# Loading the q and k rows of two tiles at a time, turning them by heads, and taking four blocks of the first product whole

## The chip, the cores and the metric

The kernel runs on one core of one Trainium2 chip. The metric is the device time of one execution in microseconds; the time quoted is the median of three runs. Engine names are those of the profile: PE is the matrix engine (PEld its weight loads), DVE the vector engine, ACT the scalar engine, POOL the GpSimd engine, SP the engine that here only issues DMAs.

## The reference

B=8 sequences of S=576 tokens; q, k and v have H=8 heads of 64. Attention stays within chunks of 64 tokens, its result (tokens by 512) goes through a gated two-layer product with a three-tap convolution over the tokens:

```
scores = 0.125 * q_c @ k_c.T             # per batch, head, chunk of 64
attn   = exp(scores - max); attn = attn / (sum(attn) + 1e-9)
x      = (attn @ v_c), heads side by side            # 4608 x 512
h      = maximum(x @ w_in, 0)                        # 512 -> 1024
conv   = sum over k of conv_w[k] * h[token + k - 1]  # zeros at each end of a batch
out    = (h * sigmoid(conv)) @ w_out                 # 1024 -> 512
```

## The kernel before

**Tiles and units.** The 4608 tokens are 36 tiles of 128 tokens (two chunks each). Four tiles make a unit of 512 tokens, u = 0 to 8. d_ff is cut into eight blocks f of 128. For each unit and block, `mm1(u, f)` (L337) makes h, and after ReLU, convolution and gate (L344 to L417) `mm2(u, j, f)` (L469) adds to the four output tiles j. Both products split each operand into a high and a low part and add three products, so a block of `mm1` over 512 tokens is 4 x 3 matmuls of 512 columns. The parts of x come from `x_hi` (L326, ACT) and `x_lo` (L329, DVE); the weights are split on the chip, in pieces of 512 or 1024 columns a partition: load L497, `w_scale` (L512, ACT), `w_shift` (L516), `w_words` (L521), then the high part (L557 and L563) and the low part (L525).

**Attention of a tile.** q and k have to stand with the head dimension on the partitions. For tiles 0 to 4 (`t < NP`) `load_rows` (L111 to L118) puts two consecutive tokens of each head into one packet of 512 bytes, q on the even partitions and k on the odd ones; `t_pe` (L169) turns them with matmuls against the identity, eight matmuls (16 records in the trace, as fp32 runs in two passes) for each half, a half being all heads of the even or of the odd tokens; `t_copy` (L189) copies each half from PSUM into the tile's `qkT` (every other element is written). Tiles 5 to 8 are loaded a token a row and turned by PE transposes (L181, copies L194); later tiles are turned by DVE (L201). Then come `scores` (L208, matmuls L215), `s_max` (L225) and `s_sub` (L229) on DVE, `s_exp` (L238) on ACT, `s_sum` (L245), `s_eps` (L248) and `s_rec` (L251) on DVE, the normalising product on POOL (L277), `p_pe` (L284) which turns the weights of attention, its copy `p_copy` (L289), `attn_v` (L303), and `x_hi` and `x_lo`.

**Unit 0.** Its `mm1` blocks are all cut into two halves of 256 columns, since the first needs only tiles 0 and 1 and the second tiles 2 and 3. Every step before the first `mm1` lies ahead of the dense stage; PE is then given small filler matmuls on the identity (L1018 with 512 columns, L1021 with 128) at places that the program works out.

**What sets the order.** Each piece of work is a `step(...)` with an engine, its predecessors, and resources that it takes and frees (PSUM banks, buffers). A table `order_` (L833) lists all steps in the order in which they are written out; `moved_` names steps that run on another engine than usual. Each engine works through its own instructions strictly in that order, and each DMA goes out through SP's queue in that order. The costs and lags in the `step` calls only set the begin times by which buffers, banks and fillers are chosen.

## Time and profile before

| what | value |
|---|---|
| median of three runs | 471.08 us (470.34, 471.23, 471.08) |
| profiled execution, its time | 470.57 us |
| profiled execution, its span | 468.8 us |
| PE busy | 460.9 us (98%) |
| DVE busy | 350.3 us (75%) |
| first `mm1` matmul starts | 27.39 us |
| last PE instruction ends | about 465.4 us |

Times in the rows are microseconds from the span's start. The busy share of PE is of records, fillers included; PE's matmuls are pipelined, so that the distance between the starts of neighbouring groups tells what a group takes, and their busy times overlap a little.

### The profile page before, as it was taken

The page shows a single profiled execution, that of the slowest core. Times are in us where ns is not written, and L with a number is a line of the kernel's source. Part 1 is how long each engine was busy: PE and PEld are TensorE (multiplying, and loading weights), DVE is VectorE, ACT ScalarE, POOL GpSimd, SP SyncE. Part 2 cuts the span into 40 slices and gives each one's busy share as a digit, 9 for nine tenths or more (in the row PEclk, how much of TensorE's full clock was granted, in tenths as well). Part 3 has the DMA queues.
Part 4 walks back from the last instruction along what each step waited for, and adds up shares of the span by engine and source line. Part 5 has one row for each costly group of instructions (what it writes and reads, how often), then busy time and mean ns, then how long its engine had stood idle before and what let it go on. Part 6 is the DMA issues. An engine that isn't in the chain of part 4 may idle for free.

```text
span 468.8 us, 10873 instructions
## 1 busy us (share of the span) xinstructions
PE 460.9 (98%) x4373; PEld 384.1 (82%) x4373; DVE 350.3 (75%) x632; ACT 226.6 (48%) x522; POOL 184.6 (39%) x256
## 2 busy tenths in 40 slices
...
GB/s 212 250 317 247 279 81 128 149 95 95 96 110 146 135 57 72 167 89 146 101 144 78 67 135 154 119 1 70 60 99 3 45 1 112 46 1 69 1 22 112
DMA packets 175638, 50.53 MB, mean 108 GB/s; under 512 B 159180, under 2 KB 167908, under 8 KB 175588
## 3 DMA queue, kind: packets, MB, share of 16 engines
...
## 4 chain that ended last, share of the span: by engine, by line
PE 89%; DVE 9%; issue 2%; ACT 0%; POOL 0%; POOLq 0%; DVEq 0%; ACTq 0%
PE b_ps L469 42%; PE b_ps L337 37%; PE b_ps L215 3%; PE b_ps L303 3%; PE b_ps L176 2%; DVE wt L521 1%; DVE x_l L329 1%; DVE z L245 1%; DVE ww L521 1%; DVE m L225 1%; DVE wi_l L525 1%; DVE c L378 1%; DVE wt L516 1%; DVE e L229 1%; DVE c L394 1%
## 5 line engine op out<-in xcount | busy, mean ns | idle before, releaser
L469 PE MATMUL b_ps<-wo_h,g_h 128*128 128x512 f32 x288 | 113.8, 395 | 0.3 <-DVE x_l L329 0.3
L469 PE MATMUL b_ps<-wo_h,g_l 128*128 128x512 f32 x288 | 112.2, 390 | 0.0
L469 PE MATMUL b_ps<-wo_l,g_h 128*128 128x512 f32 x288 | 112.2, 390 | 0.0
L417 POOL TENSOR_TENSOR g_l<-c,g_h 128x510 fp32r<-128x510 f32 (+1 forms) x80 | 79.4, 998 | 75.4 <-DVE g_h L406 48.5
L378 DVE SCALAR_TENSOR_TENSOR c<-b_ps,cw,c 128x510 f32<-128x510 f32 x72 | 53.2, 740 | 37.4 <-ACT c L373 30.8
L337 PE MATMUL b_ps<-x_h,wi_h 128*128 128x512 f32 (+1 forms) x320 | 79.8, 371 | 0.0
L337 PE MATMUL b_ps<-x_l,wi_h 128*128 128x512 f32 (+1 forms) x320 | 78.8, 368 | 0.0
L337 PE MATMUL b_ps<-x_h,wi_l 128*128 128x512 f32 (+1 forms) x320 | 78.7, 368 | 0.0
L337 PEld LDWEIGHTS b_ps<-x_h,wi_h 128*128 128x128 f32 x320 | 56.5, 188 | 10.6 <-issue 0.3
L337 PEld LDWEIGHTS b_ps<-x_l,wi_h 128*128 128x128 f32 x320 | 56.9, 188 | 10.1
L337 PEld LDWEIGHTS b_ps<-x_h,wi_l 128*128 128x128 f32 x320 | 56.9, 189 | 10.0
L469 PEld LDWEIGHTS b_ps<-wo_h,g_h 128*128 128x128 f32 x288 | 54.0, 188 | 12.4 <-DVE x_l L329 0.7
L469 PEld LDWEIGHTS b_ps<-wo_h,g_l 128*128 128x128 f32 x288 | 54.1, 188 | 11.4
L469 PEld LDWEIGHTS b_ps<-wo_l,g_h 128*128 128x128 f32 x288 | 54.1, 188 | 10.7
L373 ACT ACTIVATE c<-b_ps,cw 128x510 f32<-128x510 f32 (+1 forms) x72 | 49.8, 693 | 23.0 <-DVE b_ps L348 19.1
L344 ACT ACTIVATE b_ps<-b_ps 128x512 f32<-128x512 f32 x56 | 32.4, 584 | 55.2 <-PE b_ps L337 54.7
L260 POOL TENSOR_TENSOR wt<-wt,z 128x512 f32<-128x512 f32 x28 | 29.2, 1050 | 75.7 <-DVE z L251 28.0
L390 ACT ACTIVATE c<-c 128x510 f32<-128x510 f32 (+1 forms) x72 | 45.5, 635 | 27.7 <-DVE c L384 27.4
L394 DVE SCALAR_TENSOR_TENSOR c<-c,b_ps 128x510 f32<-128x510 f32 (+1 forms) x72 | 48.6, 678 | 10.2 <-ACT c L390 8.1
L384 DVE SCALAR_TENSOR_TENSOR c<-b_ps,cw,c 128x510 f32<-128x510 f32 (+1 forms) x72 | 53.0, 740 | 1.6 <-ACT rim L363 0.4
L201 DVE STREAM_TRANSPOSE qkT<-qk 128x512 f32<-128x512 f32 (+1 forms) x60 | 37.9, 641 | 2.8 <-DMA qk<-in_k 1.5
L326 ACT CAST x_h<-b_ps 128x512 fp32r<-128x512 f32 x36 | 20.6, 590 | 39.6 <-PE b_ps L303 36.0
...
## 6 DMA issues: line engine op xcount, KB each, us to landing
out<-os SPq DMA_DIRECT2D x35, 256.0 KB, 2.3
...
v<-in_v SPq DMA_DIRECT2D x25, 256.0 KB, 3.3
w<-in_moe_w_out SPq DMA_DIRECT2D x4, 1024.0 KB, 7.3
...
w<-in_moe_w_in SPq DMA_DIRECT2D x2, 1024.0 KB, 7.0
```

Of the source, the lines that this page charges most:

```text
L201: nc.vector.transpose(out=turned(st)[:, i].rearrange("p g (n i) -> p g n i", i=32)[:, :, to:to + n], in_=groups[b, i][:, :, n0:n0 + n, :])
L260: nc.gpsimd.tensor_tensor(out=two(st, "to"), in0=two(st, "of"), in1=z, op=ALU.mult)
L326: nc.scalar.copy(out=x_view(t, x_h), in_=x_src(st))
L337: nc.tensor.matmul(banks[st["h"]][:, c0:c1], lhsT=wt[:, f // 2, kt, P * (f % 2):P * (f % 2) + P], rhs=xt[:, u % 2, kt, c0:c1], start=n == ...
L344: nc.scalar.activation(out=h, in_=h, func=AF.Relu)
L373: nc.scalar.mul(out=st["c"], in_=banks[st["h"]][:, i0:i0 + n], mul=cw[:, FT + f:FT + f + 1])
L378: nc.vector.scalar_tensor_tensor(out=c[:, a:n], in0=banks[st["h"]][:, i0 + a - 1:i0 + n - 1], scalar=cw[:, f:f + 1], in1=c[:, a:n], op0=AL ...
L384: nc.vector.scalar_tensor_tensor(out=st["c"], in0=banks[st["h"]][:, i0 + 1:i0 + 1 + n], scalar=cw[:, 2 * FT + f:2 * FT + f + 1], in1=st["c ...
L390: nc.scalar.activation(out=st["c"], in_=st["c"], func=AF.Tanh, scale=0.5)
L394: nc.vector.scalar_tensor_tensor(out=st["c"], in0=st["c"], scalar=1.0, in1=banks[st["h"]][:, i0:i0 + n], op0=ALU.add, op1=ALU.mult)
L417: nc.gpsimd.tensor_tensor(out=g_l[:, f, gs], in0=st["c"][:, cs], in1=g_h[:, f, gs].bitcast(F32), op=ALU.subtract)
L469: nc.tensor.matmul(banks[st["o"]], lhsT=gt[:, f, o:o + P], rhs=wt[:, f, :], start=f == 0 and n == 0, stop=f == FT - 1 and n == 2)
```

## The change

Tiles 1 and 2, and tiles 3 and 4, are loaded together (`PAIRS`): a partition takes four consecutive tokens of each head, 1024 bytes in one packet, 64 partitions for q and 64 for k. The pair 3 and 4 lies across the end of a batch and is loaded in four DMAs (48 and 16 partitions each of q and of k). The pair is turned by heads: `t_pe2` makes, for a group g of two heads, eight matmuls (one for each token of four and each head) into one bank, so a pair takes four banks instead of four halves; `t_copy2` copies a bank to the `qkT` of both tiles, reading PSUM with a step of 512 bytes and writing SBUF in one run. For that the two `qkT` buffers are now two views of one tile. Tile 0 is loaded and turned as before.

Blocks f = 2 to 5 of unit 0 are taken whole (`HALVED = (0, 1, 6, 7)`): 12 matmuls of 512 columns instead of 24 of 256, which then wait for all four tiles of x. `s_eps` may run on POOL. Lags of some loads are changed (they only move the chosen begin times), and the tables `order_` and `moved_` are new throughout.

```
+    HALVED = (0, 1, 6, 7)
     NP = 5
+    PAIRS = {1: 2, 3: 4}
...
+    qk_all = spots.tile([P, G, 2, 2, 2 * C], F32, name="qkT")
+    homes["qkT"] = [qk_all[:, :, :, n].rearrange("p g i c -> p i g c") for n in range(2)]
...
-            (b0, t0), (b1, t1) = chunk(2 * t), chunk(2 * t + 1)
+            e = 4 if t in PAIRS else 2
+            (b0, t0), n0 = chunk(2 * t), min(C, (S - chunk(2 * t)[1]) // e)
             for i, src in enumerate((q, k)):
-                for b, t_, p0, n in [(b0, t0, 0, C)] if b0 == b1 else [(b0, t0, 0, C // 2), (b1, t1, C // 2, C // 2)]:
-                    nc.sync.dma_start(out=r[i, p0:p0 + n], in_=src[b, :, t_:t_ + 2 * n, :].rearrange("h (p e) d -> p h (e d)", e=2))
+                for b, t_, p0, n in [(b0, t0, 0, n0)] + [(b0 + 1, 0, n0, C - n0)] * (n0 < C):
+                    nc.sync.dma_start(out=r[i, p0:p0 + n], in_=src[b, :, t_:t_ + e * n, :].rearrange("h (p e) d -> p h (e d)", e=e))
...
+    def t_pe2(st, g):
+
+        r = row_slot(st).rearrange("p (g u e d) -> p g u e d", g=G, u=2, e=4)
+        for e in range(4):
+            for u in range(2):
+                nc.tensor.matmul(banks[st["tp", g]][D * u:D * u + D, P * e:P * e + P], lhsT=r[:, g, u, e],
+                                 rhs=ident.rearrange("p (n two) -> p two n", two=2), start=True, stop=True)
...
+    def t_copy2(st, g, copy=nc.scalar.copy):
+        for st_ in st["sts"]:
+            turned(st_)
+        copy(out=qk_all[:, g].rearrange("p i x (n e) -> p i (x n) e", e=4), in_=banks[st["tp", g]].rearrange("p (e i m) -> p i m e", e=4, i=2))
...
+    def s_eps_g(st):
+        nc.gpsimd.tensor_scalar(out=st["z"], in0=st["z"], scalar1=1e-9, scalar2=None, op0=ALU.add)
...
+        if t in PAIRS:
+            parts = 2 if C * (2 * t % NCK) + 4 * C <= S else 4
+            st["sts"] = [st]
+            ld = step("SP", 0.63 * parts, load_key, load_rows, (st, t), lag=3.4 if parts == 2 else 3.7, n=parts)
+            tt = []
+            for g in range(G):
+                s = step("PE", 1.07, key - 3, t_pe2, (st, g), [ld], behind=[before.get("t")], take=[("bk", st, ("tp", g))] + [("qkT", t), ("qkT", t + 1)] * (g == 0))
...
+                tt.append(step("ACT", 0.62, key - 3, t_copy2, (st, g), [s], free=[("bk", st, ("tp", g))], alt=[dict(eng="DVE", cost=0.68, fn=t_copy2_v)]))
...
-        s = step("DVE", 0.17, key + 2, s_eps, (st,), [s], port=True)
+        s = step("DVE", 0.17, key + 2, s_eps, (st,), [s], port=True, alt=[dict(eng="POOL", cost=0.2, fn=s_eps_g, port=True)])
...
-        if u == 0:
+        if u == 0 and f in HALVED:
             s = step("PE", 1.43, key, mm1, (st, u, f, 0, UN // 2), wi_done[f] + [x_done[0], x_done[1]], take=[("bk", st, "h")])
...
     order_ = [
-        71, 72, 90, 0, 74, 91, 1, 73, 75, 3, 2, 77, 92, 78, 4, 5, 93, 109, 94, 110,
+        71, 72, 90, 0, 17, 73, 1, 127, 74, 75, 3, 77, 91, 78, 79, 4, 2, 5, 6, 80,
...
```

The loads at the start of SP's queue, before. The buffers r_108 to r_112 are the rows of tiles 0 to 4, `os` holds the convolution weights, `c` and `v` rows of v, w_123 the first large piece of w_in.

```order
L117 DMA r_108<-in_q 64x8x128
L117 DMA r_108<-in_k 64x8x128
L117 DMA r_109<-in_q 64x8x128
L117 DMA r_109<-in_k 64x8x128
L497 DMA os_70<-in_moe_conv_w 24x256
L117 DMA r_110<-in_q 64x8x128
L117 DMA r_110<-in_k 64x8x128
L117 DMA r_111<-in_q 64x8x128
L117 DMA r_111<-in_k 64x8x128
L117 DMA r_112<-in_q 32x8x128 x2
L117 DMA r_112<-in_k 32x8x128 x2
L147 DMA c_84<-in_v 64x4x64
```

The same place of SP's queue now; r_107 is tile 0, r_108 the pair 1 and 2, r_109 the pair 3 and 4, wi_112 and w_120 pieces of w_in.

```order
L122 DMA r_107<-in_q 64x8x128
L122 DMA r_107<-in_k 64x8x128
L122 DMA r_108<-in_q 64x8x256
L122 DMA r_108<-in_k 64x8x256
L521 DMA os_70<-in_moe_conv_w 24x256
L521 DMA wi_112<-in_moe_w_in 128x2x512
L122 DMA r_109<-in_q 48x8x256
L122 DMA r_109<-in_q 16x8x256
L122 DMA r_109<-in_k 48x8x256
L122 DMA r_109<-in_k 16x8x256
L521 DMA w_120<-in_moe_w_in 128x4x512
L152 DMA c_82<-in_v 64x4x64
```

A small piece of w_in now goes ahead of tiles 3 and 4, and the first large one ahead of all rows of v; before, both came behind the first rows of v.

On ACT, before, the stretch from the second half of tile 2 to the first large piece of w_in (`e` are the weights of attention, `pT` their turned form, the copies at L192 those of tiles 0 to 4).

```order
L192 COPY qkT_72<-b_ps 128x4x2x64
L238 ACTIVATE e_77<-e_77 128x512
L192 COPY qkT_73<-b_ps 128x4x2x64
L192 COPY qkT_72<-b_ps 128x4x2x64
L289 COPY pT_80<-b_ps 128x512
L289 COPY pT_81<-b_ps 128x512
L238 ACTIVATE e_76<-e_76 128x512
L238 ACTIVATE e_77<-e_77 128x512
L326 CAST x_h<-b_ps 128x4x128
L512 ACTIVATE wt_83<-w_123 128x1024
L192 COPY qkT_72<-b_ps 128x4x2x64 x2
L194 COPY qkT_73<-b_ps 128x512
```

The same stretch of ACT now (L215 are the copies of the pairs, L259 the exponentials, L536 `w_scale`).

```order
L259 ACTIVATE e_74<-e_74 128x512
L215 COPY qkT<-b_ps 128x512 x2
L536 ACTIVATE wt_81<-wi_112 128x512
L215 COPY qkT<-b_ps 128x512
L536 ACTIVATE wt_80<-w_120 128x1024
L259 ACTIVATE e_75<-e_75 128x512
L259 ACTIVATE e_74<-e_74 128x512
L215 COPY qkT<-b_ps 128x512 x4
L350 CAST x_h<-b_ps 128x4x128
L581 CAST wi_h<-wt_80 128x1024
L313 COPY pT_79<-b_ps 128x512
L207 COPY qkT<-b_ps 128x4x128
```

The first large `w_scale` stood behind the exponentials of tiles 2 and 3; now it stands ahead of those of tiles 1 and 2 and of the four copies of the pair 3 and 4.

On PE, before, from the first filler to the turning of the attention weights of tile 0 (L176 turns rows, L215 are scores, L284 turns the attention weights, L578 belongs to the convolution weights).

```order
L1018 MATMUL b_ps<-ident 128x512
L1021 MATMUL b_ps<-ident 128x128 x10
L176 MATMUL b_ps<-ident,r_108 64x128 x16
L176 MATMUL b_ps<-ident,r_109 64x128 x8
L215 MATMUL b_ps<-qkT_72 64x64 x16
L176 MATMUL b_ps<-ident,r_109 64x128 x8
L176 MATMUL b_ps<-ident,r_110 64x128 x8
L215 MATMUL b_ps<-qkT_73 64x64 x16
L176 MATMUL b_ps<-ident,r_110 64x128 x8
L578 MATMUL b_ps<-ident,wt_82 128x24
L176 MATMUL b_ps<-ident,r_111 64x128 x16
L284 MATMUL b_ps<-ident,e_76 128x128 x4
```

The same stretch of PE now, as far as the scores of tile 3 (L181 turns tile 0, L193 a pair, L236 are scores, L327 is the product with v).

```order
L1061 MATMUL b_ps<-ident 128x512
L1064 MATMUL b_ps<-ident 128x128 x5
L181 MATMUL b_ps<-ident,r_107 64x128 x16
L1064 MATMUL b_ps<-ident 128x128
L236 MATMUL b_ps<-qkT 64x64 x16
L193 MATMUL b_ps<-ident,r_108 64x128 x32
L602 MATMUL b_ps<-ident,wt_80 128x24
L308 MATMUL b_ps<-ident,e_74 128x128 x4
L236 MATMUL b_ps<-qkT 64x64 x32
L193 MATMUL b_ps<-ident,r_109 64x128 x32
...
L236 MATMUL b_ps<-qkT 64x64 x16
```

A pair is turned in one piece, its scores follow in one piece, and fewer fillers stand ahead of tile 0.

## Rows read from the trace of the kernel before

**Rows 1.** The head of the profile's page: span, and the busy time of three engines with its share of the span and the count of instructions.

```profile
span 468.8 us, 10873 instructions
PE 460.9 (98%) x4373; PEld 384.1 (82%) x4373; DVE 350.3 (75%) x632; ACT 226.6 (48%) x522; POOL 184.6 (39%) x256
```

**Rows 2.** Busy time of each engine by stage: the stretch, its length, then for each engine its busy time and count, then the granted clock, DMA's busy share and GB/s.

```profile
5.50:27.40 21.90, 20.12 (x449) 16.83 (x448) 17.53 (x38) 13.62 (x23) 4.17 (x4) 1.00 1.00 263
27.40:65.30 37.90, 36.83 (x505) 34.23 (x503) 37.59 (x64) 31.86 (x59) 17.42 (x20) 1.00 0.83 236
65.30:440.00 374.70, 374.70 (x3302) 309.87 (x3303) 285.54 (x516) 171.54 (x420) 155.73 (x214) 1.00 0.54 89
```

**Rows 3.** The waits of PE over the whole span: the waiting line, what it waited for, the sum, how often, the longest.

```profile
PE b_ps L284 <- POOL e L277: 1.5, 2, 0.9
...
PE b_ps L215 <- ACT qkT L194: 0.4, 1, 0.4
PE b_ps L303 <- DVE pT L289: 0.4, 1, 0.4
PE b_ps L469 <- DVE x_l L329: 0.3, 1, 0.3
```

**Rows 4.** PE in order of time up to the first `mm1` matmul: start, busy time, line and operation, count of records, and in brackets the idle time before with what ended it.

```profile
3.23 2.34 PE L1021 MATMUL b_ps<-ident 128*128 128x128 f32 x10
5.50 3.28 PE L176 MATMUL b_ps<-ident,r 128*64 128x128 f32 x48
...
18.21 2.03 PE L176 MATMUL b_ps<-ident,r 128*64 128x128 f32 x32
20.18 0.55 PE L1021 MATMUL b_ps<-ident 128*128 128x128 f32 x3
21.62 0.44 PE L284 MATMUL b_ps<-ident,e 128*128 128x128 f32 x2 [0.90 <-POOL e L277]
...
23.43 0.69 PE L303 MATMUL b_ps<-pT,v 64*64 64x64 f32 x32
24.72 0.66 PE L284 MATMUL b_ps<-ident,e 128*128 128x128 f32 x4 [0.59 <-POOL e L277]
25.30 1.16 PE L215 MATMUL b_ps<-qkT 64*64 64x64 f32 x64
26.39 1.12 PE L1018 MATMUL b_ps<-ident 128*128 128x512 f32 x2
27.39 0.72 PE L337 MATMUL b_ps<-x_h,wi_h 128*128 128x256 f32 x4
```

**Rows 5.** Three loads at their issue on SP's queue (start, time of the issue): k of tile 0, k of tile 1, and the first large piece of w_in.

```profile
1.59 0.63 SPq L117 DMA_DIRECT2D r<-in_k  x1
...
2.94 0.64 SPq L117 DMA_DIRECT2D r<-in_k  x1
...
12.80 0.51 SPq L497 DMA_DIRECT2D w<-in_moe_w_in  x1
```

**Rows 6.** The same three, each in a narrow window of the DMA view: KB, and the time from issue to landing.

```profile
r<-in_k SPq DMA_DIRECT2D x1, 256.0 KB, 3.5
r<-in_k SPq DMA_DIRECT2D x1, 256.0 KB, 4.6
w<-in_moe_w_in SPq DMA_DIRECT2D x1, 1024.0 KB, 6.0
```

**Rows 7.** Three short stretches of the head, columns as in rows 2; the last number is the rate of all DMA engines. In the first the data in flight are rows of q and k, in the second mostly rows of v, in the third the first large piece of w_in and rows of tile 5.

```profile
5.10:10.00 4.90, 4.81 (x95) 4.02 (x95) 1.40 (x4) 1.65 (x3) 0.00 (x0) 1.00 1.01 287
10.00:15.00 5.00, 5.00 (x105) 4.51 (x101) 4.34 (x13) 2.91 (x6) 0.80 (x1) 1.00 1.02 197
15.00:18.00 3.00, 2.99 (x105) 2.33 (x104) 2.64 (x8) 1.52 (x4) 1.28 (x2) 1.00 1.06 360
```

**Rows 8.** Groups of ACT in the first 66 us by form: count, busy time and mean time in ns of one, idle time before.

```profile
L238 ACT ACTIVATE e<-e 128x512 f32<-128x512 f32 x8 | 5.0, 632 | 1.4 <-DVE e L229 1.3
L192 ACT COPY qkT<-b_ps 128x512 f32<-128x512 f32 x8 | 4.7, 620 | 7.2 <-PE b_ps L176 7.2
L512 ACT ACTIVATE wt<-w 128x1024 f32<-128x1024 f32 x4 | 4.6, 1152 | 0.0
...
L194 ACT COPY qkT<-b_ps 128x512 f32<-128x512 f32 x7 | 4.0, 592 | 1.3 <-PE b_ps L181 1.3
```

**Rows 9.** The low part of a piece of weights with 1024 columns, once on DVE and once on POOL, in order of time: columns as in rows 4.

```profile
36.27 1.23 DVE L525 TENSOR_TENSOR wi_l<-wt,wi_h 128x1024 fp32r<-128x1024 f32 x1
...
49.43 2.42 POOL L525 TENSOR_TENSOR wo_l<-ww,wo_h 128x1024 fp32r<-128x1024 f32 x1 [2.36 <-DVE g_h L406]
```

**Rows 10.** PE in order of time at a half block of `mm1` in unit 0 and the next, at a whole block of unit 1 and the `mm2` behind it, and at a filler.

```profile
35.52 0.64 PE L337 MATMUL b_ps<-x_h,wi_h 128*128 128x256 f32 x4
...
36.96 0.64 PE L337 MATMUL b_ps<-x_h,wi_h 128*128 128x256 f32 x4
...
47.77 0.38 PE L1021 MATMUL b_ps<-ident 128*128 128x128 f32 x2
...
69.48 1.07 PE L337 MATMUL b_ps<-x_h,wi_h 128*128 128x512 f32 x4
...
72.20 0.39 PE L469 MATMUL b_ps<-wo_h,g_h 128*128 128x512 f32 x1
```

**Rows 11.** The small fillers over the whole span: shortest, median and longest record in ns, first and last start.

```profile
L1021 PE MATMUL b_ps<-ident x16: 272/421/421, 3.2 to 47.9; 128*128 128x128 f32 x16
```

39 lines of the change are left out of this document (26 added, 13 removed), and 208 rows, old and new, of tables (moved_, order_).

## The prediction

> **What bounds the kernel now.** I read the page first: PE is busy for 460.9 of 468.8 us [rows 1], so PE's work plus what it idles is the time. The stages say where it idles [rows 2]: from 65.3 to 440 it is busy for all of 374.70 us, with DVE at 285.54 of them, and nothing there waits for another engine. Whatever the change gives or costs has to appear before 65 us, and what PE gains there shifts the rest as a block. From 27.4 to 65.3 DVE is busy for 37.59 of 37.90 us, and PE for 36.83; before 27.4 DMA has a busy share of 1.00 while PE turns rows and plays fillers. The waits of PE are small: 1.5 us for the normalising on POOL, and 0.4, 0.4 and 0.3 on three others [rows 3]. In order of time [rows 4], PE begins to turn tile 0 at 5.50 and the first `mm1` starts at 27.39; between, it is a chain of arriving rows, copies, exponentials and POOL products. So there are two questions: when does the first `mm1` start, and what does PE lose after it.
>
> **Part 1, the head.** The bytes and the PE work are the same as before: five tiles of q and k, and a pair is turned in 64 records where two tiles took 2 x 32 at 2.03 [rows 4], about 4.1 us. What moves is the arrival and the order. k of tile 0 lands at 1.59 + 3.5 = 5.1 [rows 5, 6], as it will again, since its issue does not move. The pair's 1.05 MB follow at 287 GB/s, the rate of such rows now [rows 7], at about 8.8; the second load of that size, for tile 1 alone, landed at 2.94 + 4.6 = 7.5 [rows 5, 6]. Tile 0's turning, two copies of 0.62 and its scores hold PE's chain until about 8.9 anyway, so waiting for two tiles instead of one costs nearly nothing. Then PE: pair 1-2 until 13.0, turning of tile 0's weights and the scores of both tiles (0.6 + 1.1, by the spacing in rows 4) and some waiting for POOL until 15.0, pair 3-4 (landed by then: 2.6 MB after 5.1 end at 14.2) until 19.1, tile 0's product with v until 19.7.
>
> On ACT the order decides. `w_scale` of the first large piece of w_in now stands ahead of the exponentials of tiles 1 and 2 and of the four copies of pair 3-4, and everything behind it waits for that piece to land. Ahead of its end lie 3.67 MB after 5.1: at 287 GB/s it lands at 17.9, at the 360 of the third stretch [rows 7] at 15.3. Half of what comes before it is in packets of 1 KB, half in 2 KB, none in the small packets of v that made 197 [rows 7]; I take the middle, 16.6. Then ACT, with the times of rows 8: `w_scale` 1.15 to 17.75, two exponentials at 0.63 to 19.0, four copies at 0.6 to 21.3, so that the scores of tile 3 end at 22.0 and PE idles about a microsecond for them. Behind them stand on PE, by the spacing of rows 4 and of their equals: the weights of tile 1 (0.6), tile 5's turning (1.0), tile 1's product (0.6), the weights of tile 2 (0.6), two scores (1.1), tile 2's product (0.6), together 4.5, and I add 0.5 for a wait on POOL or ACT of the size of the 0.59 and 0.90 in rows 4. First `mm1`: 27.0 against 27.39, **-0.4**. Ends: -1.7 (the piece lands at 15.3, the order of PE alone binds) and +0.9 (17.9).
>
> The copies read PSUM with a step of 512 bytes and write in one run; the present ones do the reverse and take 620 ns where an unbroken copy takes 592 [rows 8], so a step on the writing side costs 28 ns. No row has the step on the reading side. I take 0.6 each, as the nearest row; between nothing and a doubling, eight copies are to be priced, of which four lie on the chain: 0 to +2.4. [...]
>
> **Part 2, whole blocks.** A half of a block takes 36.96 - 35.52 = 1.44 us, a block in halves 2.88; a whole block takes 72.20 - 69.48 = 2.72 [rows 10]. Four blocks save 4 x 0.16 = **-0.64**. They need x of all four tiles, which the halves of f = 0 and 1 ahead of them cover, 5.8 us of PE work; if that cover is too thin, PE waits for the tile 3 product and this term is 0, not below.
>
> **Part 3, waits and fillers between 27.4 and 65.** PE loses there a filler of 0.38 [rows 10], 0.4 for a copy and 0.4 for DVE's copy of turned weights, and 0.3 for x_l at 65 [rows 3]. DVE is full in this stage, so these go only if DVE has less ahead of it. It does: both low parts of w_in with 1024 columns go to POOL, 1.23 us each on DVE, 2.42 on POOL [rows 9], one of 512 comes to DVE for it, and three `s_eps` go too; I work out some 3 us less on DVE ahead of x_l of the second unit. POOL had 17.42 of 37.90 busy [rows 2], so it has room, though its products for the attention queue behind a piece of 2.42. I take two thirds of the 1.18, **-0.8**, and two thirds of the 0.3, **-0.2**; ends 0 and -1.5 together, and a new wait for POOL of up to 1.2 is in the upper end of the head. The stream transposes of later tiles now write in runs of 512 bytes into the shared `qkT`; DVE has 89 us of slack there, so a few per cent cost nothing.
>
> Issues on SP: pair 3-4 costs four issues instead of six for its two tiles, pair 1-2 two instead of four; the piece of w_in was issued at 12.80 and is now issued ahead of v, and v's rows come later, which tile 0's product at 19.1 has to wait for if they are late; v's 0.3 MB behind the 3.67 land about 1.7 us behind the piece, at 18.3.
>
> **Sum.** -0.4 - 0.64 - 0.8 - 0.2 = -2.0 on the profiled execution's own 470.57 gives 468.5, which lies 0.51 below the median of the runs; against the median, 471.08 - 2.0 = **469.1**. By the ends alone: -3.8 and +0.9, 467.2 to 472.0.
>
> **Rivals.**
> The piece lands late: the first large piece landed at 12.80 + 6.0 = 18.8 [rows 5, 6] behind 2.95 MB. If larger packets do not run faster and the same bytes are there at the same time, the exponentials, the copies and tile 3's scores all move by 18.8 - 16.6 = 2.2: 471.3, no change. For it: nearly the same bytes stand ahead. Against: 0.3 MB of v at the low rate [rows 7] no longer stand there. Chance 0.17.
> Slow copies: reading with a step doubles the 0.6. Four copies on the chain cost 2.4, and the copies of pair 1-2 0.3: 471.8, within the bound of no change; at three times, 474.2, slower. Against it: DVE and ACT now read `(p g i)` forms without a step only, so no row tells. Chance 0.10, of which 0.03 at the slower end.
> A lower clock in the head, the one on the other side: before tile 0 PE now has five of ten small fillers, and one behind the turning. Ten took 2.34 us, at 421 ns a record against 272 later [rows 4, 11], the records of the lower of the two levels, 1.2 GHz, although the granted clock of all stretches reads 1.00 [rows 2]. With the fillers ending near 4.4 and rows at 5.3, PE idles before tile 0, and the higher level comes later. It decides if the lower level lasts beyond pair 1-2's start at 8.9: the turning of tile 0 costs 1.6 more and of the pair up to 3, less the slack of about 1 before the weights land: 473. Of this the Trainium skill (TensorE: Matmul & The Clock Gate, "What's actually happening") states that the gate lets the full clock through only after PE has been kept busy; the row of fillers agrees with that. Against it: tile 0 at the lower level is hidden in part, because ACT waits for the piece. Chance 0.08.
> The whole blocks do nothing, because PE waits for DVE as long as they save: 469.7, inside the forecast's own spread.
>
> **How the numbers follow.** The forecast with its own spread (467.4 to 470.1) has 0.60, and another 0.05 below it, where the weights land at 15.3 and all waits go. Late piece 0.17, slow copies 0.10, lower clock 0.08. The range leaves out the slow end of the copies, the clock and a little at the low end: 467.0 to 472.0. Faster or slower counts from 0.2%, 0.94 us, about what a measurement of this kernel can tell from no change: below 470.14 or above 472.02. The forecast with its low end gives 0.65, and 0.02 of the late piece falls there, so faster 0.67; the late piece and the milder copies give 0.22 of no change; slower 0.11.
>
> **What would show it.** The first `mm1` at about 27.0; the piece of w_in landing at 16 to 17, and ACT's four copies behind it, at 0.6 each, ending near 21.3; PE's wait for the scores of tile 3 about a microsecond; whole blocks of unit 0 at 2.72; no filler at 47. It is wrong if `w_scale` starts past 18.5, if the new copies take over 0.9, if the turning of pair 1-2 takes over 5 us, or if PE waits for POOL between 27 and 62.

## The result and the profile after

| | before | after |
|---|---|---|
| median of the runs on one chip | 470.76 us (470.34 to 471.23) | 474.88 us (474.22 to 475.92) |
| ratio, 95% interval | | 1.009 [1.0074, 1.0107] |
| profiled execution, its span | 470.57 us, 468.8 us | 475.92 us, 474.1 us |
| first `mm1` | 27.39 us | 32.50 us |
| first `mm1` of unit 1 | 66.07 us | 70.58 us |
| last PE instruction starts | 464.75 us | 470.04 us |

The change makes the kernel slower by about 4.1 us. The forecast was 2.0 us faster with a range up to 472.0, so both direction and range failed. The profiled execution of after is the slowest of its runs, 1.0 above their median.

The page of after, against [rows 1]: 60 matmuls fewer and PE busy 0.8 us longer, in a span that is 5.3 longer.

```profile
span 474.1 us, 10746 instructions
PE 461.7 (97%) x4313; PEld 382.4 (81%) x4313; DVE 341.5 (72%) x592; ACT 235.4 (50%) x540; POOL 194.5 (41%) x278
```

The waits of PE over the whole span, in the columns of [rows 3]. Of the four waits named there, the two of 0.4 for a copy of ACT and one of DVE are gone, that for POOL is half as long, that for x_l has grown from 0.3 to 0.5. New are 1.1 for ACT's copies of pair 3-4, 0.9 for the rows of tile 0, and the one on top; what that one waited for is "issue": no semaphore of another engine.

```profile
PE b_ps L327 <- issue: 3.0, 1, 3.0
...
PE b_ps L236 <- ACT qkT L215: 1.1, 1, 1.1
PE b_ps L181 <- DMA r<-in_k: 0.9, 1, 0.9
PE b_ps L308 <- POOL e L301: 0.7, 2, 0.4
PE b_ps L493 <- DVE x_l L353: 0.5, 1, 0.5
PE b_ps L193 <- issue: 0.5, 1, 0.5
```

PE in order of time, as [rows 4] for before (L181 turns tile 0, L193 a pair, L236 are scores, L327 the product with v, L361 `mm1`).

```profile
5.42 3.68 PE L181 MATMUL b_ps<-ident,r 128*64 128x128 f32 x32 [0.93 <-DMA r<-in_k]
...
9.80 0.69 PE L236 MATMUL b_ps<-qkT 64*64 64x64 f32 x32 [0.29 <-ACT qkT L205]
10.42 2.94 PE L193 MATMUL b_ps<-ident,r 128*64 128x128 f32 x48
13.65 1.13 PE L193 MATMUL b_ps<-ident,r 128*64 128x128 f32 x16 [0.29 <-ACT qkT L215]
...
16.99 1.13 PE L193 MATMUL b_ps<-ident,r 128*64 128x128 f32 x16
18.60 2.95 PE L193 MATMUL b_ps<-ident,r 128*64 128x128 f32 x48 [0.48 <-issue]
...
23.72 0.69 PE L236 MATMUL b_ps<-qkT 64*64 64x64 f32 x30 [1.14 <-ACT qkT L215]
...
28.66 0.69 PE L327 MATMUL b_ps<-pT,v 64*64 64x64 f32 x30
32.30 0.27 PE L327 MATMUL b_ps<-pT,v 64*64 64x64 f32 x2 [2.95 <-issue]
32.50 0.74 PE L361 MATMUL b_ps<-x_h,wi_h 128*128 128x256 f32 x4
...
34.59 1.05 PE L361 MATMUL b_ps<-x_h,wi_h 128*128 128x256 f32 x4
```

ACT in the head: `w_scale` of the large piece (L536), the exponentials behind it, the four copies of pair 3-4.

```profile
19.57 1.13 ACT L536 ACTIVATE wt<-w 128x1024 f32<-128x1024 f32 x1 [4.14 <-DMA w<-in_moe_w_in]
20.58 1.15 ACT L259 ACTIVATE e<-e 128x512 f32<-128x512 f32 x2
21.62 2.04 ACT L215 COPY qkT<-b_ps 128x512 f32<-128x512 f32 x4
```

Stretches, in the columns of [rows 2] and [rows 7]; the one from 32.50 to 70.58 runs from the first `mm1` to unit 1's.

```profile
5.10:10.00 4.90, 4.29 (x45) 3.70 (x49) 0.72 (x2) 0.61 (x1) 0.00 (x0) 1.00 0.99 316
10.00:15.00 5.00, 4.66 (x97) 4.06 (x90) 4.61 (x14) 2.71 (x6) 0.79 (x1) 1.00 1.11 231
34.00:35.00 1.00, 1.00 (x6) 1.00 (x6) 1.00 (x2) 0.39 (x1) 0.00 (x0) 0.50 1.27 292
35.00:36.00 1.00, 1.00 (x7) 1.00 (x6) 1.00 (x3) 0.81 (x2) 0.00 (x0) 0.50 1.01 186
...
32.50:70.58 38.08, 37.59 (x429) 33.10 (x428) 34.52 (x52) 30.98 (x60) 18.65 (x23) 0.96 0.72 197
```

The same stretch of before:

```profile
27.39:66.07 38.68, 37.61 (x507) 34.88 (x506) 38.37 (x65) 32.10 (x60) 18.19 (x21) 1.00 0.83 235
```

So the 5.3 us are made up of three parts. The first `mm1` comes 5.11 later; the stretch from there to unit 1 takes 0.60 less; and from unit 1's first `mm1` to the end of the span it is 403.6 us against 402.7, 0.8 more.

In the head there are four things to read. The large piece landed at 19.4 and not at 16.6, while the stretch from 10 to 15 moved 231 GB/s. ACT's copies were quick (2.04 for four) but ended at 23.66. PE then stopped for 2.95 us two matmuls before the end of tile 2's product. And after that stop the records of `mm1` take longer (1.05 a group where the same kind took 0.64 in [rows 10]), at a granted clock of 0.50, which is the lower of the two levels, 1.2 GHz; PE had done nothing from 29.35 to 32.30, and the clock fell at 33.3.

What "issue" is can be narrowed down. Ahead of 18.60 PE has 221 matmul records, ahead of 32.30 it has 475, a distance of 254. DMA queue 8, kind "instruction", moves packets of 16 KB; one starts 2.6 us ahead of the first place and one 2.5 us ahead of the second. The queue in the whole of after (packets, MB, share of the engines), and a narrow window of the DMA view, 29.6 to 29.8 us:

```profile
q8 instruction: 34, 0.56, 0.5%
```

```profile
q1 hardware_dynamic: 39, 0.08, 102.4%
q8 instruction: 1, 0.02, 29.0%
```

If these packets are all PE's, 4313 matmul records over 34 make 127 a packet, half of the 254.

This gives the theory that PE's own program arrives in pieces through the same DMA engines as the loads, and that PE ran dry. Theories for the test: **A**, the late piece of w_in and the empty instruction queue make the loss; **B**, it is the clock at tile 0 (PE's records there are as long as at the lower level, 3.68 us for 32 against 3.28 for 48 in [rows 4], though the granted clock of that stretch reads 1.00); **C**, the whole blocks or the copies cost.

### The profile page after: what moved, and what is told of

Its sections match the earlier page's. It is cut to its first block, busy times and chain, and to the rows that moved or that the text cites. A ratio compares the mean times of both kernels' runs of the same rounds, so it can differ in the third digit from the quotient of the medians.

```text
span 474.1 us, 10746 instructions
## 1 busy us (share of the span) xinstructions
PE 461.7 (97%) x4313; PEld 382.4 (81%) x4313; DVE 341.5 (72%) x592; ACT 235.4 (50%) x540; POOL 194.5 (41%) x278
## 4 chain that ended last, share of the span: by engine, by line
PE 88%; DVE 4%; DMA 2%; issue 2%; SPq 1%; ACT 1%; POOL 0%; ACTq 0%
PE b_ps L493 41%; PE b_ps L361 39%; PE b_ps L327 4%; PE b_ps L236 3%; DMA w<-in_moe_w_in 2%; SPq L122 1%; DVE wt L545 1%; DVE x_l L353 1%; DVE c L418 0%; DVE ww L545 0%; DVE c L402 0%; ACT qkT L215 0%; PE b_ps L308 0%; DVE c L408 0%; DVE wt L540 0%
## 5 line engine op out<-in xcount | busy, mean ns | idle before, releaser
L361 PE MATMUL b_ps<-x_h,wi_h 128*128 128x512 f32 (+1 forms) x304 | 80.1, 386 | 0.0
L361 PE MATMUL b_ps<-x_l,wi_h 128*128 128x512 f32 (+1 forms) x304 | 78.6, 381 | 0.0
L361 PE MATMUL b_ps<-x_h,wi_l 128*128 128x512 f32 (+1 forms) x304 | 78.4, 380 | 0.0
L361 PEld LDWEIGHTS b_ps<-x_l,wi_h 128*128 128x128 f32 x304 | 56.0, 190 | 10.9
L361 PEld LDWEIGHTS b_ps<-x_h,wi_l 128*128 128x128 f32 x304 | 56.2, 191 | 10.6
L361 PEld LDWEIGHTS b_ps<-x_h,wi_h 128*128 128x128 f32 x304 | 54.8, 190 | 10.7
L368 ACT ACTIVATE b_ps<-b_ps 128x512 f32<-128x512 f32 x59 | 34.6, 586 | 50.3 <-PE b_ps L361 49.8
L284 POOL TENSOR_TENSOR wt<-wt,z 128x512 f32<-128x512 f32 x28 | 29.3, 1052 | 20.9 <-DVE z L275 12.4
L350 ACT CAST x_h<-b_ps 128x512 fp32r<-128x512 f32 x36 | 20.6, 588 | 32.7 <-PE b_ps L327 29.6
```

Of the source, the lines that this page charges most:

```text
L284: nc.gpsimd.tensor_tensor(out=two(st, "to"), in0=two(st, "of"), in1=z, op=ALU.mult)
L350: nc.scalar.copy(out=x_view(t, x_h), in_=x_src(st))
L361: nc.tensor.matmul(banks[st["h"]][:, c0:c1], lhsT=wt[:, f // 2, kt, P * (f % 2):P * (f % 2) + P], rhs=xt[:, u % 2, kt, c0:c1], start=n == ...
L368: nc.scalar.activation(out=h, in_=h, func=AF.Relu)
```

## The experiments

Each kernel is the changed kernel with one edit unless the text says before. The table has, from the same views as above, the first `mm1`, unit 1's first `mm1`, the stretch between and PE's busy time in it, then the medians against before on the same chip. The first four columns are of one profiled execution each; in e7 and e10 that one took 2.8 and 1.7 more than the median beside it.

| kernel | first | unit 1 | between | PE busy | median us | ratio |
|---|---|---|---|---|---|---|
| before | 27.39 | 66.07 | 38.68 | 37.61 | 470.76 | 1 |
| after | 32.50 | 70.58 | 38.08 | 37.59 | 474.88 | 1.009 [1.0074, 1.0107] |
| e1_ten_fillers | 32.00 | 68.59 | 36.59 | 36.10 | 475.0 | 1.0091 [1.0071, 1.0111] |
| e2_thirty_small | 32.43 | 70.50 | 38.07 | 37.57 | 474.27 | 1.0081 [1.0061, 1.01] |
| e3_quarter_load | 31.84 | 68.44 | 36.60 | 36.09 | 473.81 | 1.0061 [1.0046, 1.0076] |
| e4_after_halves | 32.41 | 70.50 | 38.09 | 37.62 | 476.13 | 1.0119 [1.0102, 1.0136] |
| e5_before_wholes | 27.10 | 72.24 | 45.14 | 40.59 | 476.6 | 1.0128 [1.0113, 1.0143] |
| e6_load_later | 30.88 | 69.73 | 38.85 | 36.62 | 474.96 | 1.0102 [1.008, 1.0124] |
| e7_exps_first | 33.94 | 72.03 | 38.09 | 37.60 | 474.68 | 1.0104 [1.0075, 1.0132] |
| e8_v_later | 33.41 | 70.01 | 36.60 | 36.09 | 475.47 | 1.0111 [1.0094, 1.0128] |
| e9_half_packets | 31.50 | 69.61 | 38.11 | 37.62 | 474.56 | 1.0096 [1.0066, 1.0127] |
| e10_all | 31.44 | 70.08 | 38.64 | 36.66 | 473.67 | 1.0075 [1.0056, 1.0094] |
| e11_before_five | 28.62 | 67.19 | 38.57 | 37.55 | 471.11 | 1.0013 [1.0001, 1.0025] |
| e12_no_idle | 30.87 | 68.94 | 38.07 | 37.57 | 474.24 | 1.0079 [1.0066, 1.0092] |
| e13_no_idle_half | 30.23 | 68.95 | 38.72 | 36.63 | 474.1 | 1.0079 [1.0066, 1.0092] |
| e14_early_piece | 27.38 | 66.23 | 38.85 | 36.63 | 472.13 | 1.0032 [1.0018, 1.0046] |
| e15_v_held | 31.11 | 70.19 | 39.08 | 36.84 | 475.8 | 1.0107 [1.0079, 1.0134] |
| e16_one_batch | 28.67 | 67.61 | 38.94 | 36.66 | 472.65 | 1.0035 [1.002, 1.005] |
| e17_piece_first | 33.40 | 70.01 | 36.61 | 36.12 | 476.66 | 1.0129 [1.0112, 1.0146] |
| e18_piece_first_later | 33.20 | 72.33 | 39.13 | 36.65 | 477.57 | 1.014 [1.0125, 1.0156] |

### Where the wait for instructions stands

**e1_ten_fillers**: five more small fillers ahead of tile 0 (step 72).

```
+            for _ in range(5 * (i == 72)):
+                nc.tensor.transpose(out=banks[idle[-1]][:, 0:P], in_=ident, identity=ident)
```

> The changed kernel with ten small fillers ahead of tile 0 instead of five. In the changed kernel PE stands for 2.95 us in front of the last 2 of the 32 products of tile 2 with v, at 475 matmul records from the start. Theory A (PE waits for its next piece of instructions, the boundary being a fixed count of them): the wait stays about as long but now stands 5 matmuls earlier in the program, in front of the last 7 of the 32. Rival B (it waits for data, rows of v or a PSUM bank): it stays in front of the last 2. On the clock: if the five fillers that were dropped left PE at the lower level, tile 0's turning goes from 3.6 back to about 2.1 us and its scores start near 8.7 instead of 9.8; the time stays within 0.5 us of the changed kernel's 474.9, because ACT waits for the large piece of w_in until 19.6 either way. If the clock of the head binds, the time falls by 1 to 1.5.

**e2_thirty_small**: thirty transposes of 64x64 ahead of tile 3's scores (step 137).

```
+            for _ in range(30 * (i == 137)):
+                nc.tensor.transpose(out=banks[idle[-1]][0:D, 0:D], in_=ident[0:D, 0:D], identity=ident[0:D, 0:D])
```

> The changed kernel with 30 matmuls of 64x64 on the identity put in front of tile 3's scores, where PE idles 1.14 us anyway. Theory A (instruction pieces): the wait moves 30 matmuls earlier in the program, into the scores of tiles 4 and 5 (in front of the last 28 or so of the 64), and as the piece is asked for about 2 us earlier it shrinks from 2.95 to about 1 to 2 us; the time falls by 1 to 2, to 473 to 474. Rival B (data): the wait of 2.95 stays in front of the last 2 products of tile 2 with v, and the time stays at 474.9 or rises by up to 0.3.

PE at the wait in e1, and then in e2:

```profile
31.73 0.34 PE L327 MATMUL b_ps<-pT,v 64*64 64x64 f32 x7 [1.75 <-issue]
```

```profile
31.81 0.69 PE L327 MATMUL b_ps<-pT,v 64*64 64x64 f32 x32 [2.16 <-issue]
```

In after the wait stands ahead of the last 2 of the 32 matmuls. With 5 more ahead it stands ahead of the last 7, with 30 more ahead of all 32. It goes by the count of PE's instructions, not by a buffer or a semaphore. e1 also brings tile 0's turning to 2.45 us, so the clock comes up earlier; the first `mm1` is 0.5 earlier and the median no lower. Theory B falls as the main cause: tile 0 at the lower level was mostly hidden.

**e3_quarter_load**: of the second large piece of w_in only the first quarter is loaded, so that fewer bytes are under way when the packet is needed (the rest of its buffer holds a constant).

```
+        k = 1 if st.get("wslot") == 1 and not cut else n
+        nc.sync.dma_start(out=t[:, 0:k], in_=src[:, 0:k])
```

> The changed kernel, but of the 1 MB piece of w_in that is issued at 24.2 only the first quarter is loaded (the rest of its buffer is set to a constant by POOL at the start), so the weights of two blocks are not the right ones. Theory A (the piece of instructions queues behind loads): with 0.75 MB less in flight it comes earlier, PE's wait shrinks from 2.95 to 1.5 or less, the stretch at the lower clock behind it shortens too, and the time falls by 2 to 4, to 471 to 473. Rival B (rows of v of tile 2, which are issued ahead of that piece, or a bank): the wait stays near 2.95 and the time within 0.5 of 474.9.

The wait shrinks to 1.06; about a microsecond of that is PE itself coming later, the packet comes 2.0 instead of 3.5 behind it (table below). The median falls by 1.1, where 2 to 4 were expected. **e6_load_later**: that piece, whole, is issued behind v of tile 3 and the next half piece.

```
+    for i, to in [(35, 23)]:
+        line_.remove(i)
+        line_.insert(line_.index(to) + 1, i)
```

> The changed kernel with the issue of the 1 MB piece of w_in that went out at 24.2 put behind the next rows of v and the next half piece (its scaling on ACT ran only at 38.1, 4.7 us after it had landed). Theory A (PE's wait of 2.95 is for a piece of its instructions that queues behind loads): less is in flight from 24 to 28, the wait shrinks to 1 to 2 us and the time falls by 0.8 to 2, to 473 to 474. Rival B (the wait has nothing to do with the loads): no change, 474.9 within 0.4.

The wait is gone in this run. The traces have a link between packet and wait. Record 348 of PE is 127 records, a packet's worth, ahead of the one that waits:

| kernel | PE passes record 348 | packet starts | behind record 348 | PE goes on | after the packet |
|---|---|---|---|---|---|
| before (346) | 22.25 | 25.56 | 3.3 | no wait | |
| after | 26.27 | 29.77 | 3.5 | 32.30 | 2.5 |
| e2 | 25.48 | 29.38 | 3.9 | 31.81 | 2.4 |
| e3 | 27.32 | 29.35 | 2.0 | 31.64 | 2.3 |
| e9 | 25.06 | 28.70 | 3.6 | 31.25 | 2.6 |
| e14 | 23.38 | 24.79 | 1.4 | 27.10 | 2.3 |
| e6 | 27.20 | 27.56 | 0.4 | no wait | |
| e10 | 26.79 | 28.76 | 2.0 | 31.16 | 2.4 |
| e12 | 25.53 | 28.11 | 2.6 | 30.59 | 2.5 |
| e17 | 28.23 | 30.68 | 2.5 | 33.12 | 2.4 |
| e18 | 29.91 | 29.46 | -0.5 | no wait | |

Wherever PE waits there, it goes on 2.3 to 2.6 us after the packet; what changes is how late the packet comes. In the two pairs that differ in the place of the second large piece alone, it goes from 3.5 behind to 0.4 (after, e6) and from 2.5 behind to 0.5 ahead (e17, e18). But e10 and e12 have the later load too, and there the packet is 2.0 and 2.6 behind and PE waits 1.12 and 1.55; the place of that load is not all. That the packet queues behind loads is inferred from its lateness; no view shows its request.

The lateness alone doesn't make the wait. In before the packet is 3.3 us behind as well (the place is two records earlier there, at the wait "issue" of 0.18), and PE does not wait, because the next 127 records take it 6.7 us (22.25 to 29.0). In after they take 3.1 (26.27 to 29.35), since most are 64x64 records of some 20 ns. What the new order changed is the run of tiny matmuls.

Yet e6's median is no lower than after's. Two things in its trace answer for that. The granted clock fell earlier (26 to 29.4 us), behind PE's wait for tile 3's scores. And the stretch between takes 38.85 instead of the 36.6 of e1 and e3. The two waits of PE in that stretch of e6 that e1 does not have:

```profile
PE b_ps L361 <- ACT x_h L350: 0.9, 1, 0.9
PE b_ps L308 <- POOL wi_h L587: 0.7, 1, 0.7
```

The piece that was moved is issued at 29.31 instead of 24.16; on ACT its `w_scale` stands ahead of `x_h` of the next tile, and so PE waits for both. These are 1.6 of the 2.25 us; the rest is PE's busy time, 36.62 against 36.10, and small gaps. The pair e17 and e18 below tests this.

### The whole blocks

**e4_after_halves**: blocks 2 to 5 in halves again.

```
+        if u == 0 and c1 - c0 == UN:
+            mm1(st, u, f, 0, UN // 2)
+            mm1(st, u, f, UN // 2, UN)
+            return
```

> The changed kernel with blocks 2 to 5 of unit 0 taken in two halves again, one behind the other, everything else the same. If a whole block saves what the profile before told, this costs 4 x 0.16 = 0.64 us: 475.5. Rival (PE waits for DVE there, so that the saving is lost): the time stays within 0.2 of 474.9.

Its median is 1.25 above after's, but the trace gives the whole blocks less than that. From the start of block 2 to the end of block 5 PE takes 14.50 us in after (48.93 to 63.43) and 14.77 in halves, 0.27 apart. PE in after at block 2 and the step behind it, and at block 5:

```profile
48.93 1.17 PE L361 MATMUL b_ps<-x_h,wi_h 128*128 128x512 f32 x4
...
51.90 0.63 PE L308 MATMUL b_ps<-ident,e 128*128 128x128 f32 x4
...
60.71 1.07 PE L361 MATMUL b_ps<-x_h,wi_h 128*128 128x512 f32 x4
...
63.43 1.03 PE L308 MATMUL b_ps<-ident,e 128*128 128x128 f32 x8
```

Block 2 takes 2.97 from its start to the next step, in halves the same 2.97 (48.85 to 51.82 in e4); block 3, also alone between other steps, 2.98 against 2.98. Blocks 4 and 5, which stand next to each other, take 2.83 and 2.72 against 2.95 and 2.88. So a block alone between other steps wins nothing, and two neighbours win 0.12 and 0.16. The rest of the 1.25 isn't in the trace: the profiled spans of the two are equal, 474.1 us.

**e5_before_wholes**: the kernel before with blocks 2 to 5 whole, at the place of their second halves.

```
+        if u == 0 and 2 <= f <= 5:
+            if c0 == 0:
+                return
+            c0 = 0
```

> The kernel before with one part of the change alone: blocks 2 to 5 of unit 0 are taken whole at the place where their second halves stood, the first halves' places stay empty. By the spacing of the rows this saves 0.64 us, less what PE then waits for because it comes to the second halves' data sooner: 470.0 to 470.6 against 470.7. Rival (the whole blocks cost cover: PE runs dry where the first halves stood and drops to the lower clock): 471.5 or more.

Taken alone, in the old order, they cost some 6 us, as the rival in the expectation had it: PE waits 2.4 at L303 and 1.9 at L215, the granted clock is 0.50 from 48.9 to 59.1, and the stretch between takes 45.14. They need the order that came with them.

### The order on ACT, and what fills PE's idle time

**e7_exps_first**: the exponentials of tiles 1 and 2 stand ahead of the large `w_scale` on ACT.

```
+    for i, to in [(42, 117), (43, 42)]:
```

> The changed kernel with the exponentials of tiles 1 and 2 ahead of the scaling of the first large piece of w_in on ACT (and the shift on DVE behind it). Theory C (the piece lands at 19.4 and everything behind its scaling on ACT waits): the exponentials run at 18.8 to 19.9, the copies of pair 3-4 start 0.5 to 0.7 us earlier, as do tile 3's scores; tile 2's product comes as much earlier, but the wait for instructions ends where the fetch ends, so the first mm1 moves by 0 to 0.6 and the time is 474.3 to 474.9. Rival D (the piece's own chain through DVE and POOL sets the first mm1): the time stays or rises by up to 0.5.

They do start earlier (18.77), but the sums for them stand on DVE behind the shift of that same piece, so that PE waits 1.4 for POOL at tile 1's weights, and then 3.1 for instructions. Inconclusive for the ACT order alone: the order on DVE holds the same dependence.

**e10_all**: with that, the DVE shift and words behind the sums too, the later load of e6, the fillers of e1 and one large filler ahead of tile 3's scores (step 137).

```
+    for i, to in [(35, 23), (42, 117), (43, 120), (44, 43), (45, 44)]:
+            for _ in range(i == 137):
+                nc.tensor.matmul(banks[idle[-1]], lhsT=ident, rhs=..., start=True, stop=True)
+            for _ in range(5 * (i == 72)):
```

> The changed kernel with what the runs so far showed put together: ten small fillers ahead of tile 0, one filler of 512 columns in front of tile 3's scores, the later issue of the 1 MB piece (which took away the wait for instructions), and on ACT the exponentials of tiles 1 and 2 ahead of the scaling of the first large piece, with its shift and words on DVE behind the sums of both tiles. Theory (what the change lost are PE's idle stretches in the head, each paid twice, once as a wait and once more as 3.4 us at the lower clock): no wait for instructions, no stretch at the lower clock after tile 0, first mm1 at 29 to 29.7, time 470.5 to 472. Rival (the first large piece and its chain hold the first mm1 whatever PE does): first mm1 at 30.5 or later, time 473 or more.

The lowest median of the changed kernel's versions that compute everything, 473.67, and still slower than before. In the profiled execution the first `mm1` comes at 31.44, and PE waits 1.12 for instructions, which this version was to be free of. **e12_no_idle** has the later load and both kinds of fillers, without the moves on ACT and DVE.

> The changed kernel with the later issue of the 1 MB piece (no wait for instructions, in the run that had it alone), ten small fillers ahead of tile 0 and one filler of 512 columns in front of tile 3's scores, and ACT's and DVE's order as the change has it. Theory (PE's idle stretches bring it down to the lower clock for 3.4 us, which costs 1.5 to 1.9): PE is kept busy where it idled 2.2 us, no stretch at the lower clock comes after tile 0, the first mm1 starts at 29 to 29.8 (30.9 in the run with the later issue alone) and the time is 472.5 to 473.5. Rival (what bounds is the chain of the large piece of w_in, through ACT, DVE and POOL): the first mm1 stays at 30.5 or later or PE waits for x or weights behind it, and the time stays at 474.3 to 475.

The rival holds: the first `mm1` is at 30.87 and the median 474.24. The wait for instructions, expected to be gone, is back with 1.55, and the clock falls behind it.

**e11_before_five**: the kernel before with five small fillers ahead of tile 0 instead of ten.

```
+            least = pe_free + 0.14 * 5 if i == 72 else 1e9
+            while idle and pe_free + 0.14 < begin[i] - SLACK and pe_free < least - 0.01:
```

> The kernel before with five small fillers ahead of tile 0 instead of ten, as the change has it, nothing else. If the fillers are what brings PE to the higher clock before tile 0: tile 0's turning (16 matmuls, 32 records) takes about 3.5 us instead of 2.1, its scores start 1 to 1.5 later, and the time rises by 0.3 to 2, to 470.7 to 472.4. Rival (the clock of the head is hidden behind the loads): the turning is slower, the first mm1 stays at 27.4 within 0.3 and the time at 470.4 within 0.3.

The first 48 turning records take 4.58 us instead of 3.28 [rows 4], the first `mm1` comes 1.2 later, and the median rises by 0.6. So the low level at tile 0 costs something where nothing hides it, but 0.6 (0.05 to 1.2 by the interval) and not the 4.1.

### Why the large piece of w_in lands late

Three things could hold it up: the larger packets of 1 KB, v's packets behind it, or the four loads of pair 3-4.

**e9_half_packets**, on after, and **e13_no_idle_half**, on e12: the pairs' rows in packets of 512 bytes.

```
-                    nc.sync.dma_start(out=r[i, p0:p0 + n], in_=...)
+                    for a in range(0, e, 2):
+                        nc.sync.dma_start(out=r[i, p0:p0 + n, :, a * D:a * D + 2 * D], in_=...[:, :, a:a + 2])
```

> The changed kernel with each load of a pair cut in two by tokens, so that a packet holds two tokens of a head (512 bytes) as before, and lands at the same place; six more issues on SP's queue (some 3.8 us of it). Theory P (packets of 1 KB are what speeds up the loads, 316 against 287 GB/s from 5.1 to 10 us): k of pair 1-2 lands about 0.3 to 0.6 later than at 9.7, the large piece 0.5 to 1.5 later than at 19.4 and the time rises by 0.3 to 1.5. Rival Q (packets of this size cost by bytes, and the piece lands when the engines have moved the bytes ahead of it): both land within 0.2 of now, the time stays within 0.5 of 474.9.

> The kernel of the run ahead of this one with packets of 512 bytes for the pairs, as in the run with half packets, in which the large piece landed 1 us earlier. If that earlier landing is worth its time: scaling of the large piece at 18.4, first mm1 0.7 to 1 earlier than in the run ahead and the time 0.5 to 1 lower, 471.5 to 473. Rival (the landing varies by itself, whatever the packets): no difference beyond 0.4.

`w_scale` starts at 18.36 in e9 against 19.57, at 19.32 in e13 against 19.38 in e12; the medians do not move by more than their spread. Smaller packets bring the piece 1.2 earlier in one pair and 0.06 in the other, without a gain in the median. So the size of the packet isn't shown to be the cause.

**e8_v_later**: v of tile 1 behind the rows of tile 5.

```
+    for i, to in [(99, 265)]:
```

> The changed kernel with the rows of v of tile 1 issued behind the rows of tile 5 instead of ahead of them. Theory E (loads issued behind the large piece of w_in share the DMA engines with it, which is why it landed at 19.4 and not at 16.6): with 0.25 MB of small packets fewer in flight beside it, it lands 0.5 to 1 us earlier, at 18.4 to 18.9, and ACT's chain moves with it. Rival F (it lands by the bytes issued ahead of it alone): it lands at 19.4 as before. The time: 474 to 475 by either, as the wait for instructions follows.

`w_scale` starts later, at 20.65; the rows of tile 5 took v's place behind the piece, so the run tells nothing about an empty place. **e15_v_held**: e12 with v and all later loads held until the piece has landed.

```
+    tc.add_manual_dep(held[76][0], held[41][-1].name, ordered, reason="rows of v behind the landing of the piece")
```

> The kernel of the run with ten fillers, one large filler and the later issue, computing everything, with the rows of v (and with them all later loads) held back on SP's queue until the first large piece of w_in has landed. Theory (that piece landed at 19.4 because the rows of v behind it share the DMA engines, and not because of the bytes ahead of it): it lands at 16 to 17.3 and its scaling starts then; the rows of v of tile 0 land some 3.5 to 4.5 later, at 20 to 21.5, in time for tile 0's product at 20.2 or up to a microsecond late; the first mm1 starts 0.5 to 2 earlier than at 30.9. Rival (the bytes and packets ahead of it decide): its scaling starts at 18.5 or later, and everything behind it is later than now, 475 or more.

With nothing behind it the piece is no earlier (20.23). That v's packets slow it falls. The run shows something else: from 18 to 20 us only the last of the piece is under way, 27 of its 512 packets and 5 small ones, and the engines are nearly idle.

```profile
q1 hardware_dynamic: 32, 0.06, 7.5%
```

So a load lands when its last packets do, here two microseconds behind the bulk, and 7.5% is the share of about one engine of 16. Why these come so late no view shows.

**e16_one_batch**: e12, with the rows of pair 3-4 taken from one batch, in two loads of 64 partitions instead of four of 48 and 16 (other tokens, the same bytes).

```
+            if n0 < C:
+                t0, n0 = S - e * C, C
```

> The kernel of the run with ten fillers, one large filler and the later issue, but pair 3-4 is loaded in two DMAs from one batch (its last 256 tokens), where it should take 192 of them and 64 of the next batch in four DMAs; so tiles 3 and 4 get some wrong rows, and as many bytes. From 10 to 15 us, when the four DMAs run, the packets move at 231 to 239 GB/s in all, against 316 just before. Theory (the split into 48 and 16 partitions is what is slow): the rate of that stretch rises to 290 or more, the large piece lands 0.8 to 1.5 earlier than at 19.3, at 18 to 18.5, and the time falls by 0.6 to 1.5 from 474.2. Rival (the rate there is that of the whole traffic, whatever the shape of that pair's load): rate and landing stay, 474.2 within 0.4.

The stretch from 10 to 15 in e16, and the first `mm1`:

```profile
10.00:15.00 5.00, 4.35 (x74) 3.65 (x71) 4.80 (x13) 2.75 (x5) 1.04 (x1) 1.00 1.03 358
```

```profile
28.39 0.34 PE L329 MATMUL b_ps<-pT,v 64*64 64x64 f32 x8 [0.37 <-issue]
28.67 0.74 PE L363 MATMUL b_ps<-x_h,wi_h 128*128 128x256 f32 x4
```

358 GB/s instead of 239 in e12, which differs from e16 in that load alone, and 213 to 269 in the other runs that have it in this place; the share of the engines is full in all. The stretch holds packets of the piece as well. From 11 to 12 us nearly all packets under way are those of pair 3-4, 1 KB each; e12 and then e16:

```profile
DMA packets 269, 0.26 MB, mean 261 GB/s; under 512 B 14, under 2 KB 269, under 8 KB 269
q1 hardware_dynamic: 269, 0.26, 112.8%
```

```profile
DMA packets 338, 0.33 MB, mean 335 GB/s; under 512 B 11, under 2 KB 338, under 8 KB 338
q1 hardware_dynamic: 338, 0.33, 99.5%
```

By the share of 16 engines a packet takes 67 ns in e12 and 47 in e16. So the load that is split over the end of the batch is what goes slowly. Its two issues fewer also put the piece's issue at 6.09 instead of 7.97, but the engines are full in both, and in e17, where that load is split and stands behind the piece, it is as slow: 234 GB/s from 14 to 15 us. Before, only tile 4 was split, half a megabyte; as a pair, tile 3 is in the slow form too.

The piece lands at 18.3, only 1.0 earlier than in e12; the clock stays up all through, the wait for instructions is 0.37, and the first `mm1` is 2.2 earlier. So the split is about 1 of the 2.8 us by which the piece missed the forecast of 16.6; in e16 too its last packets come behind the bulk.

**e14_early_piece**: e12, and of the first large piece only the first quarter is loaded (the rest of its buffer holds a constant), so that it is there when I had forecast it.

```
+        k = 1 if st.get("wslot") == 0 and not cut else n
```

> The kernel of the run with ten fillers, one large filler and the later issue, but of the first large piece of w_in only the first quarter is loaded (the rest of its buffer is set to a constant by POOL at the start), so that two blocks have wrong weights. Theory (the landing of that piece at 19.4 and ACT's order behind it set the first mm1): it lands at 16 to 17, the exponentials of tiles 1 and 2 run as soon as DVE has their inputs (18.7), the copies of pair 3-4 end about 1.5 earlier, the first mm1 starts at 29 to 29.5 and the time falls by 1 to 2, to 472.3 to 473.3. Rival (the turning of the pairs itself, PE's chain to tile 3, sets it): the piece is early, tile 3's scores start less than 0.5 earlier and the time stays at 474.2 within 0.4.

ACT, and then PE, of e14:

```profile
16.36 1.15 ACT L542 ACTIVATE wt<-w 128x1024 f32<-128x1024 f32 x1 [1.86 <-DMA w<-in_moe_w_in]
17.78 1.29 ACT L259 ACTIVATE e<-e 128x512 f32<-128x512 f32 x2 [0.27 <-DVE e L250]
```

```profile
27.10 0.35 PE L327 MATMUL b_ps<-pT,v 64*64 64x64 f32 x9 [0.35 <-issue]
27.38 0.74 PE L361 MATMUL b_ps<-x_h,wi_h 128*128 128x256 f32 x4
...
35.56 0.74 PE L361 MATMUL b_ps<-x_h,wi_h 128*128 128x256 f32 x4 [0.92 <-ACT x_h L350]
...
47.56 0.63 PE L308 MATMUL b_ps<-ident,e 128*128 128x128 f32 x4 [0.68 <-POOL wi_h L593]
```

With `w_scale` at 16.36 the first `mm1` starts at 27.38, where 27.0 was forecast, and no stretch has the low level.

**e17_piece_first** and **e18_piece_first_later**: all of the computation, with the whole first piece issued ahead of pair 3-4, and the fillers of e12; in e18 the second large piece is moved as in e6 besides.

```
+    for i, to in [(41, 17)]:             # e17
+    for i, to in [(41, 17), (35, 23)]:   # e18
```

> The changed kernel with the first large piece of w_in issued ahead of the rows of pair 3-4, ten small fillers ahead of tile 0 and one large filler ahead of tile 3's scores; the second large piece stays where the change put it; all of the computation. If the late arrival of that piece is the cause of the late first mm1, w_scale starts at 13 to 15 instead of 19.57, pair 3-4 lands at 17 to 19, its copies end at 21.5 to 23.5, and the first mm1 starts at 27.5 to 29 plus a wait for instructions of 0 to 3 us. From there to unit 1's first mm1 it takes 36.6 as in the kernel with ten fillers, or 38.1 if PE's clock falls again, so that unit 1 begins at 64 to 68 against 66.07 before and the time is 469.5 to 473. If pair 3-4's loads are slow wherever they stand and PE's order binds, the first mm1 is at 31 as with ten fillers and no filler more, and the time is 474.

> The kernel with the first large piece ahead of pair 3-4, and its second large piece behind the rows of v of tile 3 and the next half piece. The wait for instructions at tile 2's product should be under 0.5 us, and first mm1 at 27.5 to 29. But from there to unit 1's first mm1 it should take 38.9 instead of 36.6, as in every kernel with that load moved (waits of 0.9 for x_h behind w_scale on ACT and 0.7 for POOL): unit 1 begins at 66.5 to 68, time 471.5 to 473. If those two waits come from something else than the moved load, the stage takes the same in both kernels of this pair.

ACT, PE and the stretch from the first `mm1` to unit 1's in e17:

```profile
14.59 1.19 ACT L536 ACTIVATE wt<-w 128x1024 f32<-128x1024 f32 x1 [0.56 <-PE b_ps L308]
```

```profile
19.88 5.18 PE L193 MATMUL b_ps<-ident,r 128*64 128x128 f32 x64 [4.20 <-DMA r<-in_k]
...
33.12 0.35 PE L327 MATMUL b_ps<-pT,v 64*64 64x64 f32 x9 [1.64 <-issue]
33.40 0.74 PE L361 MATMUL b_ps<-x_h,wi_h 128*128 128x256 f32 x4
```

```profile
33.40:70.01 36.61, 36.12 (x434) 31.62 (x429) 34.45 (x52) 30.98 (x60) 19.48 (x24) 1.00 0.70 191
```

The expectation for the piece holds (14.59), the one for the first `mm1` fails. Now the slow load itself is the last to come: the last of pair 3-4's loads is issued at 7.72 and lands 11.9 later, PE waits 4.2 for it, and the turning behind that takes 5.18 instead of 4.1 at a granted clock that has fallen to 0.50. Whichever of the two comes first, the other is late. The pair settles the other question: 36.61 between in e17, 39.13 in e18, so the 2.3 to 2.5 us that e6 lost there come from the place of the second large piece.

In e18 the wait for instructions is gone, as expected, and the time is still higher, 477.57. No version that I ran beats the kernel before.

## Why the prediction was wrong

**The head, the step that failed.** "Ahead of its end lie 3.67 MB after 5.1: at 287 GB/s it lands at 17.9, at the 360 of the third stretch at 15.3 ... I take the middle, 16.6." The piece landed at 7.74 + 11.7 = 19.4, outside both ends, and `w_scale` at 19.57 is past the prediction's own sign of being wrong, 18.5. Rates of other loads were put on the split load of pair 3-4. Through it 231 GB/s move from 10 to 15 us, and e16, where it is not split, has the piece 1.0 earlier; e15 excludes v, and e9 and e13 speak against the packet size. The other 1.7 or so of the 2.8 is not tied to an experiment; e15 shows that the last packets of the piece come up to two microseconds behind its bulk, which a division of bytes by a rate has no term for.

The row that spoke for the slow load was in the trace of before, the 197 of [rows 7]. The data there are not mostly rows of v, as the text beside it has it: of 0.98 MB from 10 to 15 us, 0.53 go in packets of 512 bytes, rows of q and k of tiles 3 and 4, and 0.33 in v's. From 10 to 12 v has hardly begun, and the rate is low already:

```profile
DMA packets 877, 0.42 MB, mean 212 GB/s; under 512 B 111, under 2 KB 876, under 8 KB 876
```

I gave all of it to v. What hangs on the landing went as forecast: `w_scale`, two exponentials, four copies, tile 3's scores, each in its turn, about 2.5 late. The rival "the piece lands late" had the late landing, for another reason (that larger packets run no faster), 0.17 of the chances and 2.2 us, which is near what this part cost; its time, 471.3, still had all the gains in it.

**The wait for instructions, which was in no rival.** The trace of before had a sign, in a line between those of [rows 4]; I did not ask what it was:

```profile
22.25 0.38 PE L284 MATMUL b_ps<-ident,e 128*128 128x128 f32 x2 [0.18 <-issue]
```

The working had PE's small matmuls behind tile 3's scores at their bare 4.5 us and no term for their program. The new order puts several tiles' small matmuls (turned weights, scores, products with v) into one run; it cost 2.95 us, fixed in place by e1 and e2. The packet was as late before, 3.3 us, but PE took 6.7 us for the records ahead of the place, where it now takes 3.1. The loads under way matter too: by the pairs after and e6, e17 and e18 the packet comes 3 us earlier when the second large piece comes later, but in e10 and e12 that is not enough.

**The clock.** The rival "a lower clock in the head" named the right rows, and tile 0 did take 3.68 instead of 2.0 us; but it was hidden, as the sentence against it said (e1 heals it, and the median stays). What was not foreseen is a second fall behind waits of PE: 33.3 to 36.7 in after, 23.5 to 26.9 in e1, 26.0 to 29.4 in e6, each after PE had waited two to three microseconds, in one wait (2.95 in after) or in two near each other (1.0 and 1.1 in e1). In the stretch between, it is the difference of 38.08 and 36.6: 1.5 us. In e14 and e16, where PE's longest waits are 0.5 and 1.1, there is none. The fall does not always cost as much: of e10's executions the one with it (mean granted clock 0.996) took 475.39 and the three at 1.000 took 473.4 to 473.8, but in e13 the one with it, 474.1, lies among the others.

**Waits and whole blocks, right in their sum.** Between the first `mm1` and unit 1 it takes 36.6 without a fall of the clock (e1, e3, e8, e17) against 38.68: 2.1 less where the terms gave 0.64 + 0.8 + 0.2 = 1.64. The idle part went from 1.07 to 0.49 and the filler is gone, together 0.96 of the 1.0 that I took. The term of the whole blocks was mis-sized: 0.27 by the trace in place of 0.64, since the measured 0.16 a block holds only where blocks are neighbours. Tile 2's product of 32 matmuls, some 0.6 us, stood behind the first `mm1` before (at 28.99) and is now ahead of it, where the working had it; it is in the 2.1, and is paid in the head. The turning of one tile's weights went the other way (four stand ahead of the first `mm1` before, three now), 0.35 us by the spacing at 36.97. These add up to 1.5; the other 0.6 of the 2.1 isn't accounted for, so that the sum came out near is in part luck.

**The copies** were right, and the rival "slow copies" falls. Four take 2.04 us, 0.51 apart, less than the 0.62 of [rows 8]; the seven on ACT have a mean of 594 ns. The Trainium skill (SBUF — State Buffer, the cacheline note under the port swizzle) says that any non-contiguous access pattern of PSUM, whose lines have 8 bytes, slows matmuls significantly. For copies by ACT this case shows no such cost: there the measured 594 ns decides.

**After unit 1's first `mm1`** I had put nothing: "What PE gains there shifts the rest as a block." It does not quite. From there to the end of the span it is 403.4 to 403.7 in after, e1, e3, e14, e16 and e17, and 402.7 in before, e5 and e11. The 0.8 comes with the new order whatever the head does. In the trace of after PE goes from the products into scores or products with v 18 times behind there, and 16 in before; such a visit costs some 0.24 us in its two changes (0.318 in and 0.148 out, where neighbouring products are 0.228 apart). That would be 0.5 of the 0.8; it was read and not tested.

So 2.0 faster became 5.3 slower in the profiled execution: the head -0.4 became +5.1 (about 2.5 the late piece, 2.95 the instructions), the clock +1.5, the late part +0.8, against -2.1 that held.

**Open** is why a load over 48 and 16 partitions goes slowly, why the piece's last packets trail, what in the order costs the 0.8, and why e4's median lies 1.25 above after's with an equal span. With the piece early, in e14, PE's head is as forecast and the median still 1.3 above before; there the second large piece was moved, which costs about 2.25 between. Whether it could stay in its place there without the wait for instructions coming back was not run.
